# A quadratic gate whose clamp moves to VectorE and whose square moves to ScalarE

## The chip, the cores and the metric

The kernel runs on one core of a Trainium2 chip. Its engines work side by side, each through its own queue in order: TensorE multiplies matrices from SBUF into PSUM, VectorE and ScalarE work elementwise on SBUF and PSUM, GpSimd works on SBUF, and SyncE's queue starts the DMAs. The metric is the device time of one execution in microseconds.

## What is computed

Attention over windows and summaries of keys, then a feed-forward layer with a gate that is zero up to -1, a parabola between -1 and 1, and the identity from 1 on. Cut to what matters:

```python
def _attn_ref(q, k, v):                      # 4 x 8 heads x 768 x 64
    k_sum = k.reshape(B, H, nb, block, D).max(axis=3)      # summaries of 32 keys
    v_sum = v.reshape(B, H, nb, block, D).mean(axis=3)
    ...                                      # scores within |i - j| < 16, and with the summaries
    a = np.exp(scores_all)
    a = a / (np.sum(a, axis=-1, keepdims=True) + 1e-09)
    return np.matmul(a, v_all)

def _moe_ref(x, w_in, w_out):                # x: 3072 x 512, w_in: 512 x 2048, w_out: 2048 x 512
    h = x @ w_in
    g = np.where(h >= 1, h, np.where(h <= -1, 0.0, (h + 1) ** 2 / 4))
    return g @ w_out
```

## The kernel before

The 3072 tokens are eight chunks of 384. For each chunk the attention makes the 512 rows of x, a pair of heads at a time; the feed-forward then goes through d_ff in 16 steps of 128. A step has three parts. `ff1` (F) makes h, 128 x 384, in PSUM, with 12 matmuls (line 259): x and the weights are each split in two halves, and three of the four products are summed. `gate` (G) turns h into g and splits it in `ghi` and `glo`. `ff2` (H) adds g times `w_out` to the chunk's three accumulators, with 9 matmuls (line 283); it runs two steps behind F (`LAG = 2`). There are two h buffers in PSUM (`ps_h`), so the F of a step needs the h of two steps before given back, which the gate's last reader of h, line 269, does.

The gate is five instructions on tiles of 128 x 384. Line 267 (ScalarE) writes t = relu((h + 1) / 2) from PSUM to SBUF; line 268 (VectorE) min(t, 1) * t, from SBUF to SBUF; line 269 (VectorE) the larger of h, in PSUM, and t. Line 272 (ScalarE) rounds that to `ghi`, and line 273 (GpSimd) subtracts for `glo`.

The weights come as float64. Sixteen times, 128 rows or columns of two pieces are converted: lines 99 and 110 on ScalarE, 101, 103 and 111 on VectorE, 116 on ScalarE, and 117 on GpSimd, which makes the low halves. This runs in the first 147 us, beside the attention of chunks 0 and 1 and the feed-forward of chunk 0, in an order written out by hand in the string `FIRST_CHUNK`, where F, G and H are the steps above, a, b and c the conversion, and S, E, N, T, A attention. From chunk 1 on a loop does F and G of a step, a sixteenth of the next-but-one chunk's attention (`attention`, with Exp on line 215), and H of two steps before. The text gives priorities; the order in which each engine's queue holds the instructions is a scheduler's, so between two instructions of one gate on an engine others may stand.

Of the kernel before, what the change touches and what calls it, by code (L numbers as in the profile page):

```python
# [12 lines left out]
AF = mybir.ActivationFunctionType  # L13
ALU = mybir.AluOpType
# [3 lines left out]
B, H, S, D = 4, 8, 768, 64  # L18
DM, DFF = 512, 2048
P = 128  # L20
SB = 32                 # keys in a summary
WIN = 16                # |query - key| < WIN
NSUM = S // SB          # summaries of a sequence
QB = 64                 # queries that share a window of keys
KW = QB + 2 * WIN       # keys in that window
KA = KW + NSUM          # columns of a score tile: window, then summaries
NPAIR = H // 2
T = 384                 # tokens of a chunk
NHALF = S // T
NB = T // QB            # query blocks of a chunk  # L30
NT = NB // 2            # query blocks of a score tile
NCH = B * NHALF
NK = DM // P
NF = DFF // P
NTT = T // P
W_BUFS = 3
LAG = 2                 # steps of d_ff from the first product to the second
E_BUFS = 2
FIRST_CHUNK = """
k00 m k01 v00 k02 K01 v01 R00 K00 w0 k03 S000 v02 R01 v03 E000 S001 E001 Y00 N001 N000 Y01 S010 Z00 S011 K02  # L40
# [15 lines left out]
def fused_kernel(ctx: ExitStack, tc: tile.TileContext, q2, kT, kwin, vT, vwin, w_in, w_out, mask, ident, out):  # L56
    nc = tc.nc
# [10 lines left out]

    mask_sb = const.tile([P, NT + 2, KA], F32, name="mask_sb")
    ident_sb = const.tile([P, P], F32, name="ident_sb")  # L70
    ones_half = const.tile([P, 1], F32, name="ones_half")
    nc.vector.memset(ones_half, 0.5)

# [1 line left out]
    pieces = [("win", 0), ("win", 1)] + [(n, i) for f in range(NF) for n, i in (("wout", f), ("win", f + 2)) if i < NF]  # L75
    pairs = [pieces[2 * i:2 * i + 2] for i in range(NF)]
    weight, raws, converting = {}, {}, {}

    def room(i, what, shape, dtype):
        # the 8-byte words lie where the halves will, and before them some of the first chunk's inputs  # L80
        return wpool.tile(shape, dtype, tag=f"w{i}", name=f"{what}{i}")

    def fetch(i):
# [7 lines left out]
        raws[i] = raw  # L91

    def convert_top(i):
        """float64 to float32, to nearest, then the exact split in two of 12 bits each."""
        words = raws[i].rearrange("p t n w -> p (t n) w")
        low, top = words[:, :, 0], words[:, :, 1]
        # the high word has sign, 11 exponent bits, 20 mantissa bits: as a float32, a factor of 2**-112
        # rebases the exponent, and shifted up by 3 it is the float32 but for its last 3 bits
        nc.scalar.mul(out=top.bitcast(F32), in_=top.bitcast(F32), mul=2.0 ** -112)  # L99
        w = stage.tile([P, 2 * DM], I32, tag="w", name=f"w{i}", bufs=W_BUFS)  # L100
        nc.vector.tensor_scalar(out=w, in0=top, scalar1=3, scalar2=0x7FFFFFF8,  # L101
                                op0=ALU.logical_shift_left, op1=ALU.bitwise_and)
        nc.vector.scalar_tensor_tensor(out=w, in0=top, scalar=-0x80000000, in1=w,  # L103
                                       op0=ALU.bitwise_and, op1=ALU.bitwise_or)
        converting[i] = (w, low)

    def convert_low(i):
        # the low word, rounded, gives the last 3 bits and the carry
        w, low = converting[i]
        nc.scalar.mul(out=low, in_=low.bitcast(U32), mul=2.0 ** -29)  # L110
        nc.vector.tensor_tensor(out=w, in0=w, in1=low, op=ALU.add)  # L111
# [6 lines left out]
        for part, piece in enumerate(pairs[i]):  # L118
            weight[piece] = [halves[:, h, part * DM:(part + 1) * DM] for h in range(2)]

# [1 line left out]
    ksum, vsum = {}, {}  # L122
    ins, vts, sm, pt, xs = {}, {}, {}, {}, {}

# [3 lines left out]
        tag, bufs = ("w", W_BUFS) if pool is stage else (what, 2)  # L128
        return pool.tile(shape, F32, tag=tag, name=f"{what}{c}_{p}", bufs=bufs)

    # what of the first chunk lies in the weights' rooms
    at_first = {}
    for i, share in enumerate(FIRST):
        at, at_room = 0, room(NF - 1 - i, "first", [P, 4 * DM], F32)
        for what, p in share:
            shape = {"q": [NB, P], "k": [NB, KA], "v": [NB, P]}.get(what, [S])
            flat = at_room[:, at:at + math.prod(shape)]
# [3 lines left out]
    def load_keys(c, p):  # L141
        b, hf = divmod(c, NHALF)
        if hf == 0:
            k_raw = input_tile(stage, "kraw", [P, S], c, p)
            nc.sync.dma_start(out=k_raw, in_=kT[b, p])
            raws["k", p] = k_raw
        k_t = input_tile(load, "k", [P, NB, KA], c, p)
        if c:
# [4 lines left out]

    def window_keys(c, p):
        if c == 0:
            # nothing runs yet that loads could hide behind: the windows come from what is here
            k_t = ins[c, p][1]
            eng = {"v": nc.vector, "g": nc.gpsimd}[K_COPY[p]]
            blocks = raws["k", p].rearrange("p (n q) -> p n q", q=QB)
            nc.gpsimd.memset(k_t[:, 0, :WIN], 0.0)  # L160
            eng.tensor_copy(out=k_t[:, 1:, :WIN], in_=blocks[:, :NB - 1, QB - WIN:])
            eng.tensor_copy(out=k_t[:, :, WIN:WIN + QB], in_=blocks[:, :NB, :])
            eng.tensor_copy(out=k_t[:, :, WIN + QB:KW], in_=blocks[:, 1:NB + 1, :WIN])  # L163

    def sum_keys(c, p):
        b, hf = divmod(c, NHALF)
        if hf == 0:
            ks = att.tile([P, NSUM], F32, tag=f"ks{p}", name=f"ks{b}_{p}", bufs=1)
            nc.vector.tensor_reduce(out=ks, in_=raws["k", p].rearrange("p (n j) -> p n j", j=SB), axis=AX.X, op=ALU.max)
            ksum[b, p] = ks  # L170
        nc.vector.tensor_copy(out=ins[c, p][1][:, :, KW:KA],
                              in_=ksum[b, p].unsqueeze(1).broadcast_to([P, NB, NSUM]))

    def load_vals(c, p):
# [5 lines left out]
        v_t = input_tile(load, "v", [P, NB, P], c, p)  # L180
        nc.sync.dma_start(out=v_t[:KW], in_=vwin[b, p, hf])
        vts[c, p] = v_t

    def sum_vals(c, p):
        b, hf = divmod(c, NHALF)
        if hf == 0:
            vs = att.tile([P, NSUM], F32, tag=f"vs{p}", name=f"vs{b}_{p}", bufs=1)
            nc.vector.tensor_reduce(out=vs, in_=raws["v", p].rearrange("p (n j) -> p n j", j=SB), axis=AX.X, op=ALU.add)
            vsum[b, p] = vs

    def mean_vals(c, p):
        vs_ps = ps.tile([P, 512], F32, tag="ps", name=f"vs_ps{c}_{p}")
        nc.tensor.transpose(vs_ps[:NSUM, :P], vsum[c // NHALF, p], ident_sb)  # L193
        nc.scalar.mul(out=vts[c, p][KW:KA], in_=vs_ps[:NSUM, :P].unsqueeze(1).broadcast_to([NSUM, NB, P]), mul=1.0 / SB)

    def scores(c, p, j):
        q_t, k_t = ins[c, p]
        s_ps = ps.tile([P, 512], F32, tag="ps", name=f"s_ps{c}_{p}_{j}")
        for t in range(NT):
            blk = NT * j + t  # L200
            nc.tensor.matmul(s_ps[:, t * KA:(t + 1) * KA], q_t[:, blk, :], k_t[:, blk, :], start=True, stop=True)  # L201
        e = att.tile([P, NT, KA], F32, tag=f"e{j}", name=f"e{c}_{p}_{j}", bufs=E_BUFS)
        at = c % NHALF + j
# [21 lines left out]
    def transposes(c, p, j):  # L225
        t_ps = ps.tile([P, 512], F32, tag="ps", name=f"t_ps{c}_{p}_{j}")
        for t in range(NT):
            nc.tensor.transpose(t_ps[:KA, t * P:(t + 1) * P], sm[c, p, j][0][:, t, :], ident_sb)  # L228
        pt_sb = att.tile([P, T], F32, tag=f"pt{j}", name=f"pt{c}_{p}_{j}", bufs=1)
        nc.scalar.copy(out=pt_sb[:KA], in_=t_ps[:KA, :T])  # L230
        pt[c, p, j] = pt_sb
# [15 lines left out]
        nc.vector.tensor_tensor(out=lo, in0=o_ps[:, :T], in1=hi.bitcast(F32), op=ALU.subtract)  # L247
        xs[c, p] = (hi, lo)

# [1 line left out]
    hs, gs, acc = {}, {}, {}  # L251

    def ff1(c, f):
# [8 lines left out]

    def gate(c, f):
        h_ps = hs[c, f]
        # g = max(h, min(t, 1) * t) with t = relu((h + 1) / 2)
        t_sb = gpool.tile([P, T], F32, tag="t", name=f"t{c}_{f}", bufs=2)
        nc.scalar.activation(out=t_sb, in_=h_ps[:, :T], func=AF.Relu, bias=ones_half, scale=0.5)  # L267
        nc.vector.scalar_tensor_tensor(out=t_sb, in0=t_sb, scalar=1.0, in1=t_sb, op0=ALU.min, op1=ALU.mult)  # L268
        nc.vector.tensor_tensor(out=t_sb, in0=h_ps[:, :T], in1=t_sb, op=ALU.max)  # L269
        hi = gpool.tile([P, T], F32R, tag="ghi", name=f"ghi{c}_{f}")  # L270
        lo = gpool.tile([P, T], F32R, tag="glo", name=f"glo{c}_{f}", bufs=2)
        nc.scalar.copy(out=hi, in_=t_sb)  # L272
        nc.gpsimd.tensor_tensor(out=lo, in0=t_sb, in1=hi.bitcast(F32), op=ALU.subtract)  # L273
        gs[c, f] = (hi, lo)
# [16 lines left out]
                    nc.scalar.copy(out=o_sb, in_=acc[c][i])  # L291
                nc.sync.dma_start(out=out[c * T + i * P:c * T + (i + 1) * P, :], in_=o_sb)

# [1 line left out]
    def load_constants():  # L295
        nc.sync.dma_start(out=mask_sb, in_=mask)
        nc.sync.dma_start(out=ident_sb, in_=ident)
# [1 line left out]
    steps = {  # L299
        "m": load_constants, "k": load_keys, "v": load_vals, "w": fetch,  # L300
        "K": window_keys, "R": sum_keys, "S": scores, "E": exps, "N": norms, "Y": sum_vals, "Z": mean_vals,
        "T": transposes, "A": values, "a": convert_top, "b": convert_low, "c": convert_split,
        "F": ff1, "G": gate, "H": ff2,
    }

# [2 lines left out]
            steps[step[0]](*(int(x, 16) for x in step[1:]))  # L308

    def attention(c):  # L310
        # in sixteen steps
        for p in range(NPAIR):
            if p == 0:
                do(f"k{c}{p} R{c}{p}")
            do(f"S{c}{p}0 E{c}{p}0 N{c}{p}0 S{c}{p}1 E{c}{p}1 N{c}{p}1")
            yield
            do(f"v{c}{p} Y{c}{p} Z{c}{p}")
            yield
            do(f"T{c}{p}0 T{c}{p}1")
            if p + 1 < NPAIR:  # L320
                do(f"k{c}{p + 1} R{c}{p + 1}")
            yield
            do(f"A{c}{p}")
            yield
# [74 lines left out]
```

## Time and profile before

| | us |
|---|---|
| median of 3 runs | 703.58 |
| lowest, highest | 703.25, 704.31 |
| span of the profiled execution | 703.5 |
| TensorE busy | 660.8 |
| VectorE busy | 362.4 |
| ScalarE busy | 336.4 |
| GpSimd busy | 237.3 |

The profiled execution's time is its span, from the first to the last instruction. An engine's busy time is the time in which an instruction of it was running, standing still inside an instruction included; an average over the span hides that stretches of it have different limits, so the rows below are of stretches.

### The profile page before, as it was taken

Reading aid. Unit: us, or ns where it says so; the run is one execution under the profiler, and the core shown is the slowest. Engines: PE = TensorE matmul, PEld = TensorE weight load, DVE = VectorE, ACT = ScalarE, POOL = GpSimd, SP = SyncE. Lnnn points to the kernel's source line nnn. Section 1 sums busy time; section 2 is a strip of 40 time slices with the busy share of each in tenths; the row PEclk is TensorE's granted clock in tenths of the full one; section 3 lists DMA queues with packets and bytes.
Section 4 is the critical chain, followed back from the end, with each engine's and each line's share of the span. In section 5 each row is a group of like instructions: output and inputs, shape, how many; then the busy total and the mean of one; then the engine's idle time right before and its main releaser. Section 6 shows DMA issues by size and latency. Waiting matters only on the chain.

```text
span 703.5 us, 10733 instructions
## 1 busy us (share of the span) xinstructions
PE 660.8 (94%) x4064; PEld 591.2 (84%) x4064; DVE 362.4 (52%) x671; ACT 336.4 (48%) x833; POOL 237.3 (34%) x222
## 2 busy tenths in 40 slices
PE   4858768799999999999999999999999999999997
PEld 3747667689889998989899898989899998989996
DVE  6689999956443444335444554336434443332222
ACT  4777758554444534434444544435444544433222
POOL 1336775752323232223323232223323232222221
PEclk9888988899999999999999999999999999999999
DMA  9999410136111322116212322216212320001001
GB/s 295 370 370 355 151 58 1 48 93 222 61 47 59 129 83 61 61 26 227 65 45 61 121 91 61 55 28 235 62 44 61 106 61 18 1 1 45 1 1 45
DMA packets 31379, 69.06 MB, mean 98 GB/s; under 512 B 2912, under 2 KB 11232, under 8 KB 31328
## 3 DMA queue, kind: packets, MB, share of 16 engines
q1 hardware_dynamic: 31328, 68.38, 29.9%
q8 instruction: 32, 0.52, 0.3%
q14 instruction: 19, 0.16, 0.1%
HBM read 62.07 MB, written 6.29 MB: 97 GB/s over the span
## 4 chain that ended last, share of the span: by engine, by line
PE 82%; DVE 11%; issue 3%; ACT 2%; DMA 1%; SPq 0%; POOL 0%; DVEq 0%; ACTq 0%
PE acc L283 35%; PE h L259 35%; PE s_ps L201 6%; PE o_ps L238 3%; DVE w L103 3%; PE t_ps L228 3%; DVE w L101 2%; DVE w L111 2%; DVE t L268 2%; DMA vraw<-in_vT 1%; DVE t L269 1%; ACT raw L99 1%; DVE e L204 0%; DVE nm L208 0%; PE vs_ps L193 0%
## 5 line engine op out<-in xcount | busy, mean ns | idle before, releaser
L259 PE MATMUL h<-xhi,halves 128*128 128x384 f32 x1024 | 291.6, 346 | 21.6 <-DVE t L269 20.0
L273 POOL TENSOR_TENSOR glo<-t,ghi 128x384 fp32r<-128x384 f32 x128 | 135.3, 1057 | 385.2 <-PE acc L283 187.6
L283 PE MATMUL acc<-halves,ghi 128*128 128x512 f32 x768 | 240.0, 393 | 0.0
L268 DVE SCALAR_TENSOR_TENSOR t<-t 128x384 f32<-128x384 f32 x128 | 87.0, 679 | 277.3 <-ACT t L267 277.0
L259 PEld LDWEIGHTS h<-xhi,halves 128*128 128x128 f32 x1024 | 192.2, 193 | 28.6 <-issue 17.9
L259 PE MATMUL h<-xlo,halves 128*128 128x384 f32 x512 | 175.6, 343 | 0.3 <-DVE xlo L247 0.3
L267 ACT ACTIVATE t<-h,ones_half 128x384 f32<-128x384 f32 x128 | 74.2, 581 | 211.0 <-PE h L259 211.0
L283 PEld LDWEIGHTS acc<-halves,ghi 128*128 128x128 f32 x768 | 145.3, 189 | 27.2
L283 PE MATMUL acc<-halves,glo 128*128 128x512 f32 x384 | 160.5, 418 | 0.7 <-POOL glo L273 0.7
L272 ACT CAST ghi<-t 128x384 fp32r<-128x384 f32 x128 | 65.7, 513 | 110.2 <-DVE t L269 110.1
L259 PEld LDWEIGHTS h<-xlo,halves 128*128 128x128 f32 x512 | 98.7, 193 | 5.4 <-DVE xlo L247 0.7
L283 PEld LDWEIGHTS acc<-halves,glo 128*128 128x128 f32 x384 | 72.8, 190 | 16.6 <-POOL glo L273 1.6
L215 ACT ACTIVATE e<-e,nm 128x120 f32<-128x120 f32 x192 | 73.5, 384 | 11.0 <-DVE nm L208 10.9
L269 DVE TENSOR_TENSOR t<-h,t 128x384 f32<-128x384 f32 x128 | 70.9, 554 | 3.0
L223 POOL TENSOR_TENSOR e<-e,den 128x360 f32<-128x360 f32 x64 | 55.1, 865 | 50.4 <-DVE den L222 36.7
L201 PE MATMUL s_ps<-k,q 128*128 128x120 f32 x360 | 50.2, 291 | 7.2 <-DVE k L163 5.4
L201 PEld LDWEIGHTS s_ps<-k,q 128*128 128x128 f32 x360 | 48.9, 207 | 8.2 <-issue 5.4
L117 POOL TENSOR_TENSOR halves<-w,halves 128x1024 fp32r<-128x1024 f32 x16 | 45.1, 2827 | 15.0 <-ACT halves L116 15.0
L204 DVE SCALAR_TENSOR_TENSOR e<-s_ps,mask_sb 128x360 f32<-128x360 f32 x64 | 33.6, 525 | 5.7 <-PE s_ps L201 5.5
L215 ACT ACTIVATION_READ_ACCUMULATOR e<-e,nm 128x1 f32 x192 | 35.9, 187 | 0.0
L208 DVE TENSOR_REDUCE nm<-e 128x3 f32<-128x360 f32 x64 | 33.4, 522 | 0.8
L238 PEld LDWEIGHTS o_ps<-pt,v 120*64 120x64 f32 x720 | 24.4, 141 | 10.9 <-issue 6.6
(50 smaller groups left out, 408.6 us busy)
## 6 DMA issues: line engine op xcount, KB each, us to landing
q<-in_q SPq DMA_DIRECT2D x30, 384.0 KB, 4.5
k<-in_kwin SPq DMA_DIRECT2D x28, 360.0 KB, 3.5
v<-in_vwin SPq DMA_DIRECT2D x30, 288.0 KB, 2.9
raw<-in_w_in SPq DMA_DIRECT2D x16, 512.0 KB, 9.9
raw<-in_w_out SPq DMA_DIRECT2D x16, 512.0 KB, 10.1
out<-o SPq DMA_DIRECT2D x24, 256.0 KB, 2.1
kraw<-in_kT SPq DMA_DIRECT2D x13, 384.0 KB, 3.8
vraw<-in_vT SPq DMA_DIRECT2D x13, 384.0 KB, 3.5
```

The costliest lines, as they stand in the source:

```text
L117: nc.gpsimd.tensor_tensor(out=halves[:, 1], in0=w.bitcast(F32), in1=halves[:, 0].bitcast(F32), op=ALU.subtract)
L201: nc.tensor.matmul(s_ps[:, t * KA:(t + 1) * KA], q_t[:, blk, :], k_t[:, blk, :], start=True, stop=True)
L215: nc.scalar.activation(out=e[:, t, :], in_=e[:, t, :], func=AF.Exp, bias=nm[:, t:t + 1], scale=1.0, accum_out=den[:, t:t + 1])
L223: nc.gpsimd.tensor_tensor(out=e, in0=e, in1=den.unsqueeze(2).broadcast_to([P, NT, KA]), op=ALU.mult)
L238: nc.tensor.matmul(o_ps[j * D:(j + 1) * D, blk * QB:(blk + 1) * QB], v_t[:KA, blk, j * D:(j + 1) * D], pt[c, p, blk // NT][:KA, (blk % NT) ...
L259: nc.tensor.matmul(h_ps[:, :T], weight["win", f][w][:, k * P:(k + 1) * P], x, start=(n == 0), stop=(n == 3 * NK - 1))
L267: nc.scalar.activation(out=t_sb, in_=h_ps[:, :T], func=AF.Relu, bias=ones_half, scale=0.5)
L268: nc.vector.scalar_tensor_tensor(out=t_sb, in0=t_sb, scalar=1.0, in1=t_sb, op0=ALU.min, op1=ALU.mult)
L269: nc.vector.tensor_tensor(out=t_sb, in0=h_ps[:, :T], in1=t_sb, op=ALU.max)
L272: nc.scalar.copy(out=hi, in_=t_sb)
L273: nc.gpsimd.tensor_tensor(out=lo, in0=t_sb, in1=hi.bitcast(F32), op=ALU.subtract)
L283: nc.tensor.matmul(acc[c][i], a[:, rows], weight["wout", f][w], start=(f == 0 and n == 0), stop=(f == NF - 1 and n == 2))
```

## The change

The gate becomes max(h, ((u + 1) / 2)^2) with u = h held between -1 and 1. VectorE makes u out of PSUM in place of line 268's product; ScalarE squares it in SBUF, with the halving and the added half in the same instruction, in place of line 267's ReLU; the maximum, `ghi` and `glo` stay. So the gate's instructions go VectorE, ScalarE, VectorE, ScalarE, GpSimd, where they went ScalarE, VectorE, VectorE, ScalarE, GpSimd. Their number and shapes stay. All other lines of the diff take away comments.

```diff
     def gate(c, f):
         h_ps = hs[c, f]
-        # g = max(h, min(t, 1) * t) with t = relu((h + 1) / 2)
+
         t_sb = gpool.tile([P, T], F32, tag="t", name=f"t{c}_{f}", bufs=2)
-        nc.scalar.activation(out=t_sb, in_=h_ps[:, :T], func=AF.Relu, bias=ones_half, scale=0.5)
-        nc.vector.scalar_tensor_tensor(out=t_sb, in0=t_sb, scalar=1.0, in1=t_sb, op0=ALU.min, op1=ALU.mult)
+        nc.vector.tensor_scalar(out=t_sb, in0=h_ps[:, :T], scalar1=-1.0, scalar2=1.0, op0=ALU.max, op1=ALU.min)
+        nc.scalar.activation(out=t_sb, in_=t_sb, func=AF.Square, bias=ones_half, scale=0.5)
         nc.vector.tensor_tensor(out=t_sb, in0=h_ps[:, :T], in1=t_sb, op=ALU.max)
```

## Rows read from the trace of the kernel before

**Rows 1.** Stretches: start:end, length, busy us (instructions) per engine, TensorE's clock, DMA.

```profile
40.00:150.00 110.00, 85.06 (x471) 73.39 (x467) 105.02 (x115) 74.52 (x136) 71.51 (x37) 0.88 0.45 149
150.00:700.00 550.00, 549.87 (x3423) 495.49 (x3421) 231.72 (x498) 236.22 (x628) 154.95 (x162) 1.00 0.22 70
```

**Rows 2.** Waits, 40 to 150 us: who waited for whom, us, times, longest.

```profile
PE h L259 <- DVE t L269: 20.0, 8, 5.1
```

**Rows 3.** Groups on VectorE, 40 to 150 us: busy us, mean ns, idle before.

```profile
L103 DVE SCALAR_TENSOR_TENSOR w<-raw,w 128x1024 int32<-128x1024 int32 x15 | 28.2, 1890 | 0.1
L111 DVE CUSTOM_DVE_ANT_0 w<-raw,w 128x2048 uint16<-128x2048 uint16 x15 | 22.9, 1527 | 0.3
L268 DVE SCALAR_TENSOR_TENSOR t<-t 128x384 f32<-128x384 f32 x15 | 20.5, 1367 | 4.5 <-ACT t L267 4.5
L101 DVE TENSOR_SCALAR w<-raw 128x1024 int32<-128x1024 int32 x13 | 18.1, 1398 | 0.0
```

**Rows 4.** Three lines, whole run: ns least/median/most, first and last start.

```profile
L268 DVE SCALAR_TENSOR_TENSOR t<-t x128: 521/559/2750, 44.5 to 694.4; 128x384 f32<-128x384 f32 x128
L269 DVE TENSOR_TENSOR t<-h,t x128: 539/557/560, 50.0 to 695.0; 128x384 f32<-128x384 f32 x128
L117 POOL TENSOR_TENSOR halves<-w,halves x16: 2358/2701/3377, 28.9 to 145.3; 128x1024 fp32r<-128x1024 f32 x16
```

**Rows 5.** Timeline, 126 to 135 us: start, us, instruction; then GpSimd and TensorE.

```profile
129.50 2.69 DVE L268 SCALAR_TENSOR_TENSOR t<-t 128x384 f32<-128x384 f32 x1
132.12 1.21 DVE L111 CUSTOM_DVE_ANT_0 w<-raw,w 128x2048 uint16<-128x2048 uint16 x1
133.25 0.55 DVE L269 TENSOR_TENSOR t<-h,t 128x384 f32<-128x384 f32 x1
133.72 0.68 DVE L101 TENSOR_SCALAR w<-raw 128x1024 int32<-128x1024 int32 x1
134.43 1.23 DVE L103 SCALAR_TENSOR_TENSOR w<-raw,w 128x1024 int32<-128x1024 int32 x1
...
125.97 5.81 POOL L117 TENSOR_TENSOR halves<-w,halves 128x1024 fp32r<-128x1024 f32 x2 [0.29 <-ACT halves L116]
...
133.94 0.66 PE L259 MATMUL h<-xhi,halves 128*128 128x384 f32 x1 [4.62 <-DVE t L269]
```

**Rows 6.** Groups on GpSimd, 40 to 150 us, columns as in rows 3.

```profile
L117 POOL TENSOR_TENSOR halves<-w,halves 128x1024 fp32r<-128x1024 f32 x15 | 42.7, 2858 | 15.0 <-ACT halves L116 15.0
L273 POOL TENSOR_TENSOR glo<-t,ghi 128x384 fp32r<-128x384 f32 x14 | 19.7, 1405 | 17.1 <-issue 12.1 <-ACT ghi L272 4.3 <-POOL glo L273 0.7
L223 POOL TENSOR_TENSOR e<-e,den 128x360 f32<-128x360 f32 x8 | 9.6, 1214 | 8.3 <-ACT raw L99 3.9 <-DVE den L222 2.3 <-DVE k L171 2.1
```

**Rows 7.** Timeline of the end, GpSimd and TensorE.

```profile
696.25 1.01 POOL L273 TENSOR_TENSOR glo<-t,ghi 128x384 fp32r<-128x384 f32 x1 [3.17 <-ACT ghi L272]
...
697.67 0.39 PE L283 MATMUL acc<-halves,glo 128*128 128x512 f32 x1
```

**Rows 8.** Groups of VectorE and ScalarE, whole run, columns as in rows 3.

```profile
L289 DVE COPY o<-acc 128x512 f32<-128x512 f32 x8 | 5.5, 682 | 3.7 <-PE acc L283 3.7
...
L272 ACT CAST ghi<-t 128x384 fp32r<-128x384 f32 x128 | 65.7, 513 | 110.2 <-DVE t L269 110.1
L246 ACT CAST xhi<-o_ps 128x384 fp32r<-128x384 f32 x32 | 15.3, 478 | 8.9 <-PE o_ps L238 8.9
...
L215 ACT ACT_TABLE_LOAD x1 | 1.3, 1283 | 0.7 <-PEq L388 0.7
```

**Rows 9.** Timeline around 304 us, ScalarE, VectorE and TensorE.

```profile
303.44 0.58 ACT L267 ACTIVATE t<-h,ones_half 128x384 f32<-128x384 f32 x1 [1.86 <-PE h L259]
304.05 0.56 DVE L268 SCALAR_TENSOR_TENSOR t<-t 128x384 f32<-128x384 f32 x1 [3.02 <-ACT t L267]
304.64 0.56 DVE L269 TENSOR_TENSOR t<-h,t 128x384 f32<-128x384 f32 x1
...
311.15 0.33 PE L259 MATMUL h<-xhi,halves 128*128 128x384 f32 x1
```

## The prediction

> **What bounds the kernel now.** I read the table of stretches first [rows 1]. It cuts the run in three. [...] From 40 to 150 us TensorE is busy only 85.06 of 110 us, at a mean clock of 0.88, while VectorE is busy 105.02 of 110. (Up to 40 us the transfers rule, and no gate has run.) So one engine, VectorE, sets the pace of this middle stretch, and only there can a change of the gate move the end.
>
> The waits of the stretch say how [rows 2]: the first product (L259) waits 20.0 us, in 8 pieces, for the gate's last step on VectorE (L269), because that step gives an h buffer back and there are two.
>
> Then, what fills VectorE there [rows 3]: the three steps of the weight conversion (L103, L111, L101) and the gate's L268, whose 15 instructions take 1367 ns on the mean, 20.5 us. For ScalarE's first step L268 waits there only 4.5 us. The same instruction takes 559 ns as the median of the whole run, at most 2750 [rows 4]. So 20.5 - 15 x 0.56 = 12.1 us of it is standing still, though counted as busy. The next gate step, L269, works on the same shape and never left 539 to 560 ns [rows 4]. What differs: L268 reads two operands from SBUF (t twice), L269 reads one from PSUM and one from SBUF.
>
> What it stands still for is seen in one place [rows 5]: L268 starts at 129.50, while GpSimd's pair of L117 runs from 125.97 to 131.78, and ends at 132.19, 0.4 us behind it; L111 follows, L269 only at 133.25, and TensorE starts the first product at 133.94 after 4.62 us of waiting. So instructions of VectorE that read SBUF twice, and the conversion steps (L103: 1.23 us alone, 1890 ns on the mean [rows 3, 5]), take turns with GpSimd's L117, L273 and L223 [rows 6]. Added at their undisturbed lengths [rows 3 to 7]: L103 15 x 1.23 = 18.5, L111 15 x 1.21 = 18.2, L101 13 x 0.68 = 8.8, L268 15 x 0.56 = 8.4, L117 15 x 2.36 = 35.4, L273 14 x 1.01 = 14.1, together 103.4 us, and L223 up to 9.6 more: 103 to 113 of the 110 us. The turns of the two engines explain the whole stretch.
>
> **The change, part by part.** *L267 goes from ScalarE to VectorE as a clamp out of PSUM.* It takes L268's place on VectorE: one SBUF operand fewer, nothing that takes turns with GpSimd. Its length isn't in the trace; the nearest rows are the copy from PSUM, 682 ns for 512 columns [rows 8], so for 384 between 512 (pro rata) and 682, and L269, 539 to 560 for the very shape with one operand in PSUM [rows 4]. I take L269's 0.55 us, with 0.51 and 0.68 as ends (2 us for 15 of them, at the upper end). Outside the middle stretch that is L268's median again: nothing.
> [...]
>
> What the lost turns are worth has two sides. At most the 12.1 us of standing still; by the sum of turns it is the 8.4 us that L268 no longer claims, since the next conversion step inherits what is left of GpSimd's instruction; at least nothing, if that step inherits all of it. I take 8 us, the sum of turns, as it accounts for the stretch.
>
> *L268 goes from VectorE to ScalarE as the square.* It reads SBUF where the old first step read PSUM: the casts at 513 ns from SBUF and 478 from PSUM [rows 8] give 35 ns more than the old activation's 0.58 us, so 0.58 to 0.62; 128 of them are 4.5 us of ScalarE, of which 0.5 us fall between 40 and 150, where ScalarE has 74.52 of 110 us to do [rows 1]. Off the path: nothing.
>
> *A crossing is added.* VectorE's chain was first step (ScalarE), then two steps on VectorE; now VectorE clamps, ScalarE squares, VectorE takes the maximum. If the maximum stands right behind the clamp in VectorE's queue, VectorE idles for the square and two hand-overs. Of these one takes 0.03 us (L267 ends at 304.02, L268 starts at 304.05 [rows 9]), so it idles some 0.7 us, 10 us for 15 gates, and behind it wait the conversion and the scores of the next chunk. But the queues aren't in the order of the program: another instruction stands between L268 and L269 in the place shown (L111 [rows 5]), and in 13 of the 14 gates up to 145 us. An instruction of over 0.7 us there hides the square. ScalarE, with a third of the stretch to spare [rows 1], will mostly be free when the clamp ends. I take 2 us, three exposed squares, from 0 to 10.
>
> *The steady part.* The gate's latency grows by a hand-over and at most 0.1 us of lengths. Around 304 us L269 has given h back at 305.20 and the first product that needs the buffer starts at 311.15 [rows 9]: nearly 6 us of cover. Nothing is late. If the cover were gone, each 0.1 us would count in every one of the some 110 gates, 11 us.
>
> *The end.* The last glo (L273) is done at 697.26, the product that needs it starts at 697.67 [rows 7]: 0.4 us of cover for a gate that is 0.1 us longer. Nothing, at most 0.2.
>
> **Sum.** -8 + 2 = -6 us against the profiled execution, whose span is 703.5; the median of the runs, 703.58, is the same within 0.1. So 697.5 us. It must come out of the 20.0 us that TensorE waits for L269, and there is room. Upside: after the 4.62 us wait L259 took 0.66 us for its first instruction, where it takes 0.33 in the steady part [rows 5, 9], and the granted clock is 0.88 on the stretch's mean where it is 1.00 without pauses [rows 1]; with two long waits fewer, some 2 us each return. With the 12.1 us, and no exposed square, the time is near 690.
>
> **The rivals.** *The standing still is handed on.* The step behind the clamp is one of the conversion, it meets the same L117, and VectorE gains only work it does beside. For it: the conversion steps stand still already (L103's 28.2 us hold 15 x (1.89 - 1.23) = 10 us of it [rows 3, 5]). Against: L117 no longer waits for L268 either. Gain 0 to 1: 703.
>
> *The maximum comes late (slower).* What stands between clamp and maximum is a conversion step, and with the square to wait for, one more is put in front of the maximum. Each is 1.2 us, 1.5 to 1.9 with its own standing still, and h is held that much longer, with TensorE behind it. For it: TensorE's 8 waits end with L269 [rows 2], and VectorE's queue is never empty. Against: VectorE's total falls, so all that is queued comes earlier. It decides if more than five of the eight gates get such a step (8 / 1.5); at all eight it is 8 x 1.5 - 8 = +4: 707.5, up to 711.
>
> *The square needs another activation table than the exponential.* The trace has one load, 1283 ns [rows 8], for Exp, ReLU and copies. If the square were in another table, each of the 8 groups of Exp in the middle stretch (one to each L223 [rows 6]) would bring up to two loads: 20.5 us for ScalarE, 95 of 110 us, of which I'd see half on the path: 697.5 + 10 = 707.5; the steady part covers 1.3 us. [...]
>
> **How the numbers follow.** Less time through fewer turns: 0.62, own range 690 to 701.5. Handed on: 0.16, 702 to 704.5. Maximum late: 0.18, 705 to 711. Table loads: 0.04. A measurement of this kernel tells 0.2%, 1.4 us, from no change. Faster 0.63, same 0.16, slower 0.21. The range for 8 in 10 takes the first two cases and the near part of the third: 690 to 706.5.
>
> **What would show it.** Right: between 40 and 150 us the clamp takes 0.51 to 0.60 us each time, also beside L117; VectorE's busy time there falls by over 8 us; the first product waits under 14 us for the gate; the conversion (last L117 at 145.3 us before [rows 4]) ends 5 us or more earlier; the steady part is as long as before. Handed on: L101, L103 and L111 have longer means by what L268 lost. Late: VectorE idle in front of the maximum, or two conversion steps between clamp and maximum, and a wait of the first product over 20 us. Table loads: more than one in the trace. I'd be wrong altogether if the steady part shows TensorE waiting.

## The result and the profile after

The changed kernel takes 697.49 us (median of 4 runs, 697.41 to 697.97), the kernel before 703.85 beside it: a ratio of 0.9915, 95% interval 0.9901 to 0.9929. The forecast was 697.5.

Where the time went is in the table of stretches, the columns as in [rows 1]:

```profile
40.00:150.00 110.00, 90.83 (x504) 78.21 (x505) 100.40 (x124) 77.34 (x143) 74.92 (x39) 0.91 0.45 151
150.00:690.00 540.00, 540.00 (x3363) 487.21 (x3362) 234.18 (x487) 232.83 (x619) 151.57 (x160) 1.00 0.22 70
```

In the middle stretch TensorE does 5.8 us more in the same 110 us than before, and at a mean clock of 0.91 instead of 0.88; from 150 us on it is full, as it was. The spans are 703.5 and 696.0, 7.5 us apart; 0.7 us of it is no work of the change, as the profile of the kernel before starts its first L117 at 28.9 us, the other at 28.2, ahead of every gate. What TensorE and VectorE wait for in that stretch (answering [rows 2]):

```profile
PE h L259 <- DVE t L269: 11.4, 6, 3.0
...
PE h L259 <- POOL halves L117: 2.1, 1, 2.1
...
PE acc L283 <- POOL glo L273: 1.3, 2, 0.8
...
DVE t L267 <- PE h L259: 6.5, 3, 3.1
DVE w L101 <- POOL halves L117: 2.2, 1, 2.2
DVE t L269 <- ACT t L268: 0.3, 1, 0.3
```

TensorE waits 11.4 us for the gate, where it waited 20.0. For the square, VectorE waits 0.3 us in all. The groups of VectorE in the stretch (answering [rows 3]):

```profile
L103 DVE SCALAR_TENSOR_TENSOR w<-raw,w 128x1024 int32<-128x1024 int32 x14 | 29.0, 2074 | 0.1
L111 DVE CUSTOM_DVE_ANT_0 w<-raw,w 128x2048 uint16<-128x2048 uint16 x15 | 22.5, 1502 | 0.3
L101 DVE TENSOR_SCALAR w<-raw 128x1024 int32<-128x1024 int32 x13 | 18.9, 1464 | 2.2 <-POOL halves L117 2.2
L267 DVE TENSOR_SCALAR t<-h 128x384 f32<-128x384 f32 x17 | 9.2, 544 | 6.5 <-PE h L259 6.5
L269 DVE TENSOR_TENSOR t<-h,t 128x384 f32<-128x384 f32 x17 | 9.1, 544 | 0.4 <-ACT t L268 0.3
```

The clamp, now line 267, takes 544 ns on the mean where L268 took 1367. L103 and L101 have become longer by 184 and 66 ns. Over the whole run (least, median, most, answering [rows 4]), the clamp and the last L117:

```profile
L267 DVE TENSOR_SCALAR t<-h x128: 522/558/559, 43.4 to 686.3; 128x384 f32<-128x384 f32 x128
...
L268 ACT ACTIVATE t<-t,ones_half x128: 587/617/625, 44.4 to 686.8; 128x384 f32<-128x384 f32 x128
...
L117 POOL TENSOR_TENSOR halves<-w,halves x16: 2361/2824/3407, 28.2 to 138.1; 128x1024 fp32r<-128x1024 f32 x16
```

No clamp is over 559 ns. One place beside GpSimd, answering [rows 5] (timeline: start, us, instruction):

```profile
118.62 2.87 DVE L101 TENSOR_SCALAR w<-raw 128x1024 int32<-128x1024 int32 x1 [2.24 <-POOL halves L117]
121.41 0.54 DVE L267 TENSOR_SCALAR t<-h 128x384 f32<-128x384 f32 x1
121.87 2.93 DVE L103 SCALAR_TENSOR_TENSOR w<-raw,w 128x1024 int32<-128x1024 int32 x1
124.72 0.55 DVE L267 TENSOR_SCALAR t<-h 128x384 f32<-128x384 f32 x1
...
115.27 8.46 POOL L117 TENSOR_TENSOR halves<-w,halves 128x1024 fp32r<-128x1024 f32 x3
```

While GpSimd runs L117 without a break from 115.27 to 123.73, the clamp at 121.41 takes its plain 0.54 us, and the L103 behind it, 1.2 us long undisturbed, takes 2.93 and ends at 124.80. That is the change in small: the clamp passes, the conversion step behind it inherits the rest. The L101 in front of the clamp shows something that the prediction's "two operands from SBUF" leaves out: it is of the clamp's kind, a TENSOR_SCALAR with one input, but its input is in SBUF, and it takes 2.87 us there for the 0.68 of [rows 5].

### The profile page after: what moved, and what is told of

Read it like the earlier page. It is cut to its first block, busy times and chain, and to the rows that moved or that the text cites. A ratio compares the mean times of both kernels' runs of the same rounds, so it can differ in the third digit from the quotient of the medians.

```text
span 696.0 us, 10776 instructions
## 1 busy us (share of the span) xinstructions
PE 658.7 (95%) x4064; PEld 588.9 (85%) x4064; DVE 361.6 (52%) x671; ACT 337.3 (48%) x833; POOL 237.3 (34%) x222
## 4 chain that ended last, share of the span: by engine, by line
PE 83%; DVE 10%; issue 2%; ACT 2%; DMA 1%; POOL 1%; DVEq 0%; ACTq 0%; SPq 0%
PE h L259 35%; PE acc L283 35%; PE s_ps L201 6%; PE o_ps L238 3%; PE t_ps L228 3%; DVE w L103 2%; DVE w L111 2%; DVE w L101 2%; ACT raw L99 1%; DVE t L267 1%; DVE e L204 1%; DVE t L269 1%; DMA v<-in_vwin 1%; DVE ks L169 1%; POOL halves L117 0%
## 5 line engine op out<-in xcount | busy, mean ns | idle before, releaser
L259 PE MATMUL h<-xhi,halves 128*128 128x384 f32 x1024 | 290.3, 344 | 15.1 <-DVE t L269 11.4
L273 POOL TENSOR_TENSOR glo<-t,ghi 128x384 fp32r<-128x384 f32 x128 | 138.0, 1079 | 383.6 <-ACT ghi L272 195.5
L267 DVE TENSOR_SCALAR t<-h 128x384 f32<-128x384 f32 x128 | 71.0, 555 | 210.0 <-PE h L259 161.0
L268 ACT ACTIVATE t<-t,ones_half 128x384 f32<-128x384 f32 x128 | 78.7, 617 | 185.6 <-DVE t L267 184.9
L223 POOL TENSOR_TENSOR e<-e,den 128x360 f32<-128x360 f32 x64 | 52.3, 820 | 46.4 <-DVE den L222 30.6
L230 ACT COPY pt<-t_ps 120x384 f32<-120x384 f32 x64 | 30.0, 476 | 44.8 <-PE t_ps L228 44.8
L117 POOL TENSOR_TENSOR halves<-w,halves 128x1024 fp32r<-128x1024 f32 x16 | 45.4, 2847 | 13.8 <-ACT halves L116 13.8
```

Of the source, the lines that this page charges most:

```text
L117: nc.gpsimd.tensor_tensor(out=halves[:, 1], in0=w.bitcast(F32), in1=halves[:, 0].bitcast(F32), op=ALU.subtract)
L223: nc.gpsimd.tensor_tensor(out=e, in0=e, in1=den.unsqueeze(2).broadcast_to([P, NT, KA]), op=ALU.mult)
L259: nc.tensor.matmul(h_ps[:, :T], weight["win", f][w][:, k * P:(k + 1) * P], x, start=(n == 0), stop=(n == 3 * NK - 1))
L267: nc.vector.tensor_scalar(out=t_sb, in0=h_ps[:, :T], scalar1=-1.0, scalar2=1.0, op0=ALU.max, op1=ALU.min)
L268: nc.scalar.activation(out=t_sb, in_=t_sb, func=AF.Square, bias=ones_half, scale=0.5)
```

## The experiments

Each time is a median, beside runs of the kernel before on the same chip (704.14 to 704.49). In every one the scheduler also moved some instructions in the queues, so differences of a microsecond are not read. The changed kernel was not run again beside them; its 697.49 us goes with the 703.85 above.

**One operand of the old step from PSUM.** The old division between the engines stays; only where L268 reads from is changed.

```diff
-        nc.vector.scalar_tensor_tensor(out=t_sb, in0=t_sb, scalar=1.0, in1=t_sb, op0=ALU.min, op1=ALU.mult)
+        nc.vector.scalar_tensor_tensor(out=t_sb, in0=h_ps[:, :T], scalar=1.0, in1=t_sb, op0=ALU.min, op1=ALU.mult)
```

> The kernel before, with one operand of L268 taken from h in PSUM instead of t in SBUF: min(h, 1) * t, so the gate's lower branch is not the reference's. Engines, number and shapes of the instructions stay. Theory of turns (L268 stood still because it read SBUF twice while GpSimd worked): L268 takes 0.52 to 0.60 us every time, none over 0.7; time 695 to 699 us. Rival of order (the gain came from the gate's new division between ScalarE and VectorE and the queues' new order): L268 may shorten, but the time stays 702 to 705.

Measured: 697.07 us, ratio 0.9907 (0.9893 to 0.9922), the same as the whole change within a microsecond. L268 in it:

```profile
L268 DVE SCALAR_TENSOR_TENSOR t<-h,t x128: 521/557/559, 44.6 to 686.3; 128x384 f32<-128x384 f32 x128
```

At most 559 ns, where the same form with both operands in SBUF reached 2750 [rows 4]. So the operand is the cause of L268's standing still, and with it alone the whole gain is there: the gate's new division between the engines neither gains nor costs more than a microsecond. The rival of order falls in the form that was put, with its 702 to 705 us. But VectorE's queue was reordered here too, so this run alone doesn't say how much of the 7.1 us is order; the tied pair below, whose queues differ in few places, is the closer test. Why L101 stands still with one input from SBUF (2.87 us for 0.68), no run here shows.

**An extra instruction, both operands in SBUF or one in PSUM.** First a pair on the changed kernel, with an instruction behind the clamp whose result nobody uses (`spare` is a constant tile; the second of the pair has `in0=h_ps[:, :T]`):

```diff
         nc.vector.tensor_scalar(out=t_sb, in0=h_ps[:, :T], scalar1=-1.0, scalar2=1.0, op0=ALU.max, op1=ALU.min)
+        nc.vector.scalar_tensor_tensor(out=junk, in0=spare, scalar=1.0, in1=spare, op0=ALU.min, op1=ALU.mult)
```

> The changed kernel with one more VectorE instruction behind each clamp: 128 x 384, the form of the old L268, both operands a constant tile in SBUF, its result used by nobody. Theory of turns: up to 150 us its 15 or so instructions stand still beside GpSimd as L268 did (mean over 1.0 us, most over 2.5), so 8 us of turns come back and the 8 us of new work lie in them: 702 to 708 us. Rival of VectorE's time alone (only the sum of its busy work counts): the same as the kernel with the operand in PSUM, within 1 us.

> As the one before, but the extra instruction reads h in PSUM and a constant tile in SBUF. Theory of turns: 0.52 to 0.60 us each, never longer; it adds 8 us of VectorE's own time up to 150 us, which lie partly beside GpSimd's turns: 698 to 702.5 us, at least 3 us less than with both operands in SBUF. Rival of VectorE's time alone: no difference between the two, both near 705.

Measured: 720.33 us and 708.53, neither in its range. The first decides nothing, since its extra instruction depends on nothing and the scheduler moved it: the busy time of VectorE on the extra tile, up to 40 us and from there to 150, in the columns of a table of stretches cut to VectorE:

```profile
0.00:40.00 40.00, 12.99 (x22) 0.90 0.99 352
40.00:150.00 110.00, 6.79 (x5) 0.85 0.42 145
```

13 us of it lay ahead of the middle stretch, and the first clamp starts at 47.0 us instead of 43.4. The second stayed in place, and it is a miss of mine: 14 instructions of 541 ns that take no turns cost 11 us, not 0.5 to 5. Not all of that is VectorE's load: VectorE is busy 97.69 of the 110 us in it, less than the 100.40 of the changed kernel, and waits 4.9 us for the square, where that waits 0.3. So the pair was made again, tied to the clamp's result, so that it can't move; the two differ in the operand `in0` only.

```diff
+        nc.vector.scalar_tensor_tensor(out=junk, in0=t_sb, scalar=1.0, in1=t_sb, op0=ALU.min, op1=ALU.mult)
```

```diff
+        nc.vector.scalar_tensor_tensor(out=junk, in0=h_ps[:, :T], scalar=1.0, in1=t_sb, op0=ALU.min, op1=ALU.mult)
```

> The changed kernel with one more VectorE instruction between clamp and square, tied to the clamp: 128 x 384, both operands the clamped tile in SBUF, the result used by nobody; the square waits until it has read. Theory of turns: it stands still as the old L268 did, mean over 1.1 us up to 150 us, and the time is 5 to 12 us over that of the kernel whose extra instruction reads h in PSUM: 713 to 720 us. Rival of VectorE's time alone: the same as that kernel within 1 us.

> As the one before, but one operand of the extra instruction is h in PSUM. Theory of turns: 0.52 to 0.56 us each time; VectorE's own time and the later square cost what the untied one did, 706 to 711 us.

Measured: 712.25 us with two operands in SBUF, 706.76 with one in PSUM. The extra instruction up to 150 us, in the first and in the second (groups: busy us, mean ns, idle before):

```profile
L269 DVE SCALAR_TENSOR_TENSOR junk<-t 128x384 f32<-128x384 f32 x13 | 16.2, 1242 | 0.0
```

```profile
L269 DVE SCALAR_TENSOR_TENSOR junk<-h,t 128x384 f32<-128x384 f32 x14 | 7.6, 544 | 0.0
```

With two SBUF operands it stands still as the old L268 did: 13 x (1242 - 559) = 8.9 us; the times differ by 5.5. So the cost of turns comes back with the operand, here at some six tenths of the standing still. The first came out a little under its forecast (713 to 720). The second, forecast after the miss, says the same as the untied one: 7.6 us of VectorE's own time in 14 places, and a square that much later, cost 9.3 us; no run parts the two.

**Without the clamp.** The square straight from PSUM, one VectorE instruction less.

```diff
-        nc.vector.tensor_scalar(out=t_sb, in0=h_ps[:, :T], scalar1=-1.0, scalar2=1.0, op0=ALU.max, op1=ALU.min)
-        nc.scalar.activation(out=t_sb, in_=t_sb, func=AF.Square, bias=ones_half, scale=0.5)
+        nc.scalar.activation(out=t_sb, in_=h_ps[:, :T], func=AF.Square, bias=ones_half, scale=0.5)
```

> The changed kernel without the clamp: ScalarE squares (h + 1) / 2 straight from PSUM, so h beyond -1 and 1 is not the reference's. VectorE has one instruction of 0.55 us per gate less, that takes no turns; a hand-over less. Theory of turns (the stretch up to 150 us is filled by VectorE's and GpSimd's turns): little gain, 694 to 697.5 us. Rival of VectorE's time alone: 15 x 0.55 = 8 us less, 689 to 691.

Measured: 695.42 us, 2.1 under the changed kernel, though 17 x 0.54 = 9.2 us of VectorE's work are gone. TensorE's waits in the middle stretch show what is late then:

```profile
PE h L259 <- DVE t L268: 5.8, 3, 3.6
PE acc L282 <- POOL glo L272: 5.7, 4, 2.2
PE h L259 <- POOL halves L117: 2.9, 1, 2.9
```

Of the waits in these rows 8.6 us are now for GpSimd, where the changed kernel has 3.4. Taking VectorE's own time away is worth little, and by these waits it is because GpSimd is next; putting some on, between the clamp and the maximum, costs all of it and more.

**The partner taken away.** L117, the weights' subtraction, on VectorE instead of GpSimd, once with the old gate and once with the new.

```diff
-        nc.gpsimd.tensor_tensor(out=halves[:, 1], in0=w.bitcast(F32), in1=halves[:, 0].bitcast(F32), op=ALU.subtract)
+        nc.vector.tensor_tensor(out=halves[:, 1], in0=w.bitcast(F32), in1=halves[:, 0].bitcast(F32), op=ALU.subtract)
```

> The kernel before, with the weights' subtraction of L117 on VectorE instead of GpSimd. Theory of turns with L117 as the main partner: L268 is left only L273 and L223 to stand still for, so its mean up to 150 us falls from 1.37 to 0.6 to 0.8 us and its most to under 1.6; VectorE gets 18 us of work and loses more than that of standing still: 690 to 702 us. Rival (L268 was slow in this stretch for another reason, transfers or the conversion as such): its mean stays over 1.2 us.

> The changed kernel, with the same move of L117 to VectorE. Theory of turns: with the partner gone the change is worth less: 0 to 4 us below the kernel before with the same move, against 6.4 us without it. Rival of order: it stays at 6 us.

Measured: 692.95 us with the old gate (0.9843, 0.9826 to 0.9859), 693.00 with the new (0.9846, 0.9828 to 0.9863). The change of the gate is worth nothing there. With the old gate, L268 and L117 over the whole run:

```profile
L268 DVE SCALAR_TENSOR_TENSOR t<-t x128: 524/559/1152, 44.2 to 682.8; 128x384 f32<-128x384 f32 x128
```

```profile
L117 DVE TENSOR_TENSOR halves<-w,halves x16: 1206/1215/2045, 32.0 to 132.4; 128x1024 fp32r<-128x1024 f32 x16
```

The most of L268 falls from 2750 to 1152 ns, so GpSimd's instructions of 2.4 us and more were its main partner. Both kernels also beat the changed one by 4.5 us: L117 takes 1.2 us on VectorE where it took 2.4 to 3.4 on GpSimd, and VectorE, which takes on that work, no longer stands still for it. VectorE's groups up to 150 us with the old gate:

```profile
L117 DVE TENSOR_TENSOR halves<-w,halves 128x1024 fp32r<-128x1024 f32 x15 | 21.1, 1415 | 0.0
L103 DVE SCALAR_TENSOR_TENSOR w<-raw,w 128x1024 int32<-128x1024 int32 x14 | 19.3, 1383 | 0.0
L111 DVE CUSTOM_DVE_ANT_0 w<-raw,w 128x2048 uint16<-128x2048 uint16 x15 | 18.6, 1242 | 0.0
L101 DVE TENSOR_SCALAR w<-raw 128x1024 int32<-128x1024 int32 x13 | 11.8, 924 | 0.0
L268 DVE SCALAR_TENSOR_TENSOR t<-t 128x384 f32<-128x384 f32 x18 | 11.0, 613 | 4.9 <-ACT t L267 4.9
```

L103, L111, L101 and L268 take 60.7 us where they took 89.7 [rows 3], so 21.1 us of L117 are more than paid for.

**A part of the partner.** With the new gate, L117 on VectorE for every second pair of pieces, and for three in four (`nc.gpsimd if i % 4 == 3 else nc.vector`).

```diff
-        nc.gpsimd.tensor_tensor(out=halves[:, 1], in0=w.bitcast(F32), in1=halves[:, 0].bitcast(F32), op=ALU.subtract)
+        (nc.vector if i % 2 else nc.gpsimd).tensor_tensor(out=halves[:, 1], in0=w.bitcast(F32), in1=halves[:, 0].bitcast(F32), op=ALU.subtract)
```

> The changed kernel, with L117 on VectorE for every second pair of pieces, on GpSimd for the others. Theory of turns: with half of the partner gone, between 697.5 us (all on GpSimd) and 693.0 (all on VectorE), or a little under both if VectorE's own time is what binds once the turns are few: 690 to 696 us. The rival, that the place of L117 doesn't matter beyond VectorE's load: 697 or more.

> The same with one pair in four on GpSimd, three on VectorE: 690 to 695 us by the theory of turns, near the kernel with all on VectorE.

Measured: 698.95 us for the half, a miss, and 693.58 for the three quarters. The half lies where its rival put it (697 or more); the three quarters, and all of it, speak against that rival. Moving half of the partner is worth nothing, the next quarter nearly all. In the profile of the half VectorE's steps are between (L103 at 1642 ns), but TensorE waits 5.8 us for glo, 4.0 of it once, and 9.5 for the gate:

```profile
PE h L259 <- DVE t L269: 9.5, 5, 4.3
PE acc L283 <- POOL glo L273: 5.8, 3, 4.0
```

The time doesn't follow the standing still in proportion. Whether the queues' new order or the mixture as such does this stays open; no run has a fixed order.

## Why the prediction was right, step by step

*The bound.* Right: the middle stretch gave it, and the steady part is full before and after: from 150 us on TensorE is busy 549.87 of 550 us [rows 1] and 540.00 of 540, at a granted clock of 1.00 in both. Up to 40 us the DMA share is 0.99 before and 1.00 after.

*The cause.* Right for L268, and shown: its second SBUF operand against GpSimd's L117. The operand alone gives 697.07 us; with the partner gone the change gives 0; put back on a tied instruction, the operand costs 5.5. As the difference that tells who stands still, two operands in SBUF are too narrow: L101 has one.

*The lost turns, -8.* Nearly right in size, by a sum that is too simple. The operand alone gave 7.1 us (704.14 to 697.07). Of the 12.1 us of standing still some 5 were handed on: L103 14 x 0.184 = 2.6, L101 13 x 0.066 = 0.9, and L221, a 128 x 3 step, 8 x 0.25 = 2.0 (155 to 407 ns), less 0.4 of L111. 12.1 - 5.1 = 7.0. That this meets the 7.1 is partly chance, since the window holds different work in the two kernels; over the same work, the sixteen conversions, L101, L103 and L111 take 76.0 us where they took 73.6, and the 16 of L221 up to 150 us 4.8 where they took 2.7, together 4.5 handed on. So my first rival, handing on, was part of what happened. The sum of turns called the stretch filled by the two engines' turns, and from that it followed that VectorE's other work lies beside them. That step failed: 14 instructions without a turn cost 9 to 11 us. A chain fits better, from VectorE's conversion over ScalarE to GpSimd and back into VectorE's queue by way of the gate (in the changed kernel ScalarE's L116 waits 8.2 us for L111, GpSimd's L117 13.8 for L116, the clamp 6.5 for TensorE): in it VectorE's own time and the gate's latency count, and GpSimd stands close behind, which would be why taking time away returns 2.1. That the added time counts is shown; the chain is read from the waits only.

*The crossing, +2.* Mis-sized: VectorE waited 0.3 us for the square. With the crossing 697.49, without 697.07. Both terms were off by under 2 us, in opposite directions; that the sum then met the measured time to 0.01 us is luck.

*The clamp.* 0.55 forecast, 0.544 measured in the stretch. A longer time for the PSUM source doesn't show: 558 ns is the clamp's median, and the same instruction L268 has a median of 559 with both operands in SBUF [rows 4] and 557 with one in PSUM.

*The square.* 0.58 to 0.62 us forecast, 617 ns the median, off the path.

*The maximum comes late.* It did in places (from the clamp at 94.67 to the maximum at 103.19 lie eight other instructions), yet TensorE's wait for the gate fell to 11.4 us, while VectorE's queue as a whole came earlier.

*The tables.* The 0.04 for this rival was my estimate. One load in the trace, as before:

```profile
L215 ACT ACT_TABLE_LOAD x1 | 1.3, 1283 | 0.7 <-PEq L388 0.7
```

*The signs that I named.* The first product's wait under 14 us: 11.4. The last L117 5 us earlier or more: 138.1 for 145.3, of which 0.7 lay ahead of the gates. VectorE's busy time in the stretch was to fall by over 8 us and fell by 4.6, and more of the run's work now lies in the same 110 us (17 gates instead of 14 or 15); the sign was badly chosen, a fixed window isn't a fixed piece of work.

*The base.* I took span and time for the same. The changed kernel's profiled execution took 697.97 us with a span of 696.0, so some 2 us lie outside the span. An execution of the kernel before with the span that I started from, 703.5, took 705.25 us beside the experiments, so the profiled one was some 1.4 us longer than the median, and it is chance that its span lay within 0.1 us of the median time. The spans differ by 7.5 us, the times by 6.4. Counted from the median of the runs, 703.58, the sum gives 697.6, so the forecast stands.

## What to carry to other kernels

When an elementwise instruction's mean is far over its median, look at what the other engines run in those moments before you look at its dependencies: here 12 us of standing still were counted as busy time. Moving one operand to PSUM cured the one instruction (at most 559 ns where it had reached 2750), but the rest of its wait went in part to the next instruction of the same kind (L103, 184 ns longer on the mean); taking the long partner off GpSimd brought the kernel 11 us under the one before, with either gate, where the new gate alone brought 6.4. Read the worth of an engine's time in both directions: here 9 us less brought 2, and 8 us more, put into the gate, cost 9 to 11.

## What the runs showed of the hardware

The subtraction of 128 x 1024 takes 2.36 us on GpSimd and 1.21 on VectorE, both at their shortest. I hadn't expected that its price on GpSimd was mostly paid by VectorE: with the subtraction moved to VectorE, four other groups of VectorE's take 29 us less.

Instructions with one SBUF operand stood still too, a small step among them. L221 (128 x 3, one input, 155 ns on the mean before) has a mean of 407 ns in the changed kernel: three of its eight take 0.54 to 0.99 us, and each of these ends 0.02 or 0.03 us behind an L273 of GpSimd. One of them, from the timeline of VectorE and of GpSimd:

```profile
104.93 0.96 DVE L221 TENSOR_SCALAR den<-den 128x3 f32<-128x3 f32 x1
...
104.69 1.17 POOL L273 TENSOR_TENSOR glo<-t,ghi 128x384 fp32r<-128x384 f32 x1 [2.95 <-issue]
```

L101, one input too, takes 0.68 us where GpSimd is idle and up to 2.87 beside L117; the clamp, the same kind of instruction with its input in PSUM, never took over 559 ns.
